# A one-column bias per row maximum: from GpSimd to VectorE

## The chip, the cores and the metric

The kernel runs on one core of a Trainium2 chip. The metric is the device time of one execution in microseconds (us). Ratios below are the mean time of one kernel's fast runs over that of the other's fast runs of the same rounds, so they are not quite the ratio of the medians quoted beside them. Engines: PE is TensorE (PEld its weight loads), DVE is VectorE, ACT is ScalarE, POOL is GpSimd, SP is SyncE, which issues most DMAs (388 of the 455 on the page of before; GpSimd 64).

## The reference

Attention over 8 batches, 8 heads, 576 rows and columns, head size 64, in which only scores within `tau` of the row's maximum count, followed by two matrix products with a hard-swish between them:

```python
scores = scale * q @ k.T
thresh = max(scores, axis=-1) - tau
scores = where(scores >= thresh, scores, -1e9)
attn   = exp(scores - max(scores)) / sum(...)
x      = attn @ v                          # to (4608, 512)
h      = x @ w_in
out    = (h * clip(h + 3, 0, 6) / 6) @ w_out
```

## The kernel before

A main loop of 144 slots works on two 128x576 score tiles per slot. In slot n the softmax of slot n runs beside the exponentials of slot n-1, one piece of the first matrix product, one of the second, and the scores of slot n+1. From slot 22 on the matrix products fill PE (97% busy from 100 to 500 us); slots 0 to 21 (here "the head") are attention alone.

```python
def sm_max(sl):                            # VectorE: copy out of PSUM with row maximum; then the bias
    ...
    for i, ps in enumerate(sl.tiles):
        nc.vector.tensor_scalar(out=sl.s[:, i, :]..., in0=ps[:, :, 0:HALF], scalar1=1.0, scalar2=None,
                                op0=Alu.mult, op1=Alu.max, accum_out=sl.m[:, i:i + 1])
        nc.gpsimd.tensor_scalar(out=sl.bias[:, i:i + 1], in0=sl.m[:, i:i + 1], scalar1=-scale, scalar2=tau,
                                op0=Alu.mult, op1=Alu.add)

def sm_mask(sl, i):                        # ScalarE: needs the bias
    nc.scalar.activation(out=s, in_=s, func=Act.Prelu, bias=sl.bias[:, i:i + 1], scale=scale, alpha=REJECT)

def sm_norm(sl):                           # GpSimd: two 128x576 normalizations, then a DMA transpose
    ...

for n, sl in enumerate(queue):             # one slot
    ...                                    # exponentials of slot n-1 (ScalarE)
    sm_max(sl)
    ...                                    # first product -> relu -> gate; reciprocal of n-1; second product
    for i in range(2):
        sm_mask(sl, i)
    ...                                    # transposes or attn @ v; scores of slot n+1
    sm_norm(prev)
    start(loads, 1)                        # q, k of later slots: issued by SyncE
    if n < 4 or n > 12:
        start(vcasts, 1)                   # one load of V:       issued by GpSimd
    if n > 3:
        start(casts, 1 if n < 24 else 2)   # pieces of the weights: issued by GpSimd
```

GpSimd's instructions start in the order of the program. There are two score banks in PSUM (one per tile) and one `h` bank: the next scores wait for this slot's maxima (PE sat idle 2.8 us for them in all), and the next piece of the first product waits for the gate (5.0 us).

Of the kernel before, what the change touches and what calls it, by code (L numbers as in the profile page):

```python
# [21 lines left out]
def kernel(  # L22
# [10 lines left out]
    nc = tc.nc  # L33
# [11 lines left out]
    scale = 1.0 / math.sqrt(D)  # L45
    tau = float(tau)
# [227 lines left out]
    def sm_max(sl):  # L274
        sl.s = s_pool.tile([P, 2, S], F32, tag="s", name="s")
        sl.m = stat_pool.tile([P, 2], F32, tag="m", name="m")
        sl.bias = stat_pool.tile([P, 2], F32, tag="bias", name="bias")
        sl.rsum = stat_pool.tile([P, 2], F32, tag="rsum", name="rsum")
        sl.rinv = stat_pool.tile([P, 2], F32, tag="rinv", name="rinv")
        for i, ps in enumerate(sl.tiles):  # L280
            nc.vector.tensor_scalar(out=sl.s[:, i, :].rearrange("p (a b) -> p a b", a=2), in0=ps[:, :, 0:HALF],  # L281
                                    scalar1=1.0, scalar2=None, op0=Alu.mult, op1=Alu.max,
                                    accum_out=sl.m[:, i:i + 1])
            nc.gpsimd.tensor_scalar(out=sl.bias[:, i:i + 1], in0=sl.m[:, i:i + 1], scalar1=-scale, scalar2=tau,  # L284
                                    op0=Alu.mult, op1=Alu.add)

    def sm_mask(sl, i):
# [142 lines left out]
    for quad in range(NQUAD):  # L430
        for slot in range(NSLOT):
            sl = Slot()
# [6 lines left out]
    for n, sl in enumerate(queue):  # L439
# [13 lines left out]
        if prev is not None:  # L453
            for i in range(2):
                sm_exp(prev, i)
        sm_max(sl)

        if slot != 8 and todo1:
# [148 lines left out]
```

## Time and profile before

| | |
|---|---|
| time | 560.16 us median of 4 (559.52 to 560.89) |
| profiled span | 558.7 us, granted clock 0.996 |
| PE, DVE, ACT, POOL busy | 95%, 76%, 84%, 55% |
| bias on GpSimd | 288 instructions of 189 ns |
| ScalarE's wait for it | 35.2 us |

The lines themselves stand in the prediction. Lines from the timeline have the columns: start, duration, engine and line, operation, names, shapes, and in brackets the idle time before it and what ended it.

### The profile page before, as it was taken

Reading aid. Unit: us, or ns where it says so; the run is one execution under the profiler, and the core shown is the slowest. Engines: PE = TensorE matmul, PEld = TensorE weight load, DVE = VectorE, ACT = ScalarE, POOL = GpSimd, SP = SyncE. Lnnn points to the kernel's source line nnn. Section 1 sums busy time; section 2 is a strip of 40 time slices with the busy share of each in tenths; the row PEclk is TensorE's granted clock in tenths of the full one; section 3 lists DMA queues with packets and bytes.
Section 4 is the critical chain, followed back from the end, with each engine's and each line's share of the span. In section 5 each row is a group of like instructions: output and inputs, shape, how many; then the busy total and the mean of one; then the engine's idle time right before and its main releaser. Section 6 shows DMA issues by size and latency. Waiting matters only on the chain.

```text
span 558.7 us, 11624 instructions
## 1 busy us (share of the span) xinstructions
PE 530.6 (95%) x3829; PEld 309.2 (55%) x3870; DVE 424.7 (76%) x1041; ACT 469.7 (84%) x999; POOL 305.3 (55%) x646
## 2 busy tenths in 40 slices
PE   8899798799999999999999999999999999999997
PEld 6655455555555555655555555655555565654663
DVE  3787686787878788887978788887978798883440
ACT  4899899798889999899898999899898999984440
POOL 2788878854556555755556555755556555561000
PEclk9999899999999999999999999999999999999999
DMA  5999979976789869978689889977689865454102
GB/s 121 137 120 173 196 128 190 204 142 126 137 158 152 152 136 157 178 149 146 130 148 152 173 131 160 175 147 147 131 145 166 150 144 114 100 109 94 38 20 76
DMA packets 286348, 77.52 MB, mean 139 GB/s; under 512 B 269264, under 2 KB 281808, under 8 KB 286288
## 3 DMA queue, kind: packets, MB, share of 16 engines
q1 hardware_dynamic: 267680, 67.47, 65.3%
q0 software_dynamic: 17408, 8.92, 13.6%
q8 instruction: 30, 0.49, 0.4%
q10 hardware_dynamic: 1200, 0.39, 0.3%
q14 instruction: 30, 0.25, 0.1%
HBM read 36.70 MB, written 9.44 MB: 83 GB/s over the span
## 4 chain that ended last, share of the span: by engine, by line
PE 55%; DVE 11%; ACT 8%; issue 4%; SPq 3%; DMA 2%; POOL 2%; DVEq 0%; POOLq 0%
PE h L357 17%; PE o L386 16%; PE s L260 15%; DVE s L281 5%; PE av L327 3%; ACT s L289 3%; ACT s L294 3%; DMA nq<-in_q_dram 2%; DVE g L374 2%; DVE r L368 2%; ACT r L366 1%; PE s L266 1%; PE tp L214 1%; SPq L310 1%; POOL pn L302 1%
## 5 line engine op out<-in xcount | busy, mean ns | idle before, releaser
L302 POOL TENSOR_SCALAR pn<-s,rinv 128x576 bf16<-128x576 f32 x288 | 211.6, 745 | 133.1 <-DVE rinv L297 57.3
L289 ACT ACTIVATE s<-s,bias 128x576 f32<-128x576 f32 x288 | 206.9, 766 | 36.3 <-POOL bias L284 35.2
L281 DVE TENSOR_SCALAR_CACHE_REDUCE s<-s 128x576 f32<-128x576 f32 x288 | 205.9, 752 | 40.3 <-PE s L260 29.9
L294 ACT ACTIVATE s<-s 128x576 f32<-128x576 f32 x288 | 192.7, 671 | 0.3
L260 PE MATMUL s<-kT,qT 64*128 64x288 f32 x1024 | 169.7, 430 | 5.1 <-DVE s L281 2.8
L357 PE MATMUL h<-xT,w_in_sb 128*128 128x320 bf16 (+1 forms) x1024 | 144.9, 287 | 5.9 <-DVE g L374 5.0
L386 PE MATMUL o<-w_out_sb,g 128*128 128x512 bf16 x535 | 133.5, 379 | 5.2 <-DVE osb L394 3.0
L357 PEld LDWEIGHTS <-w_in_sb 128*128 128x128 bf16 x1024 | 92.1, 97 | 68.9 <-issue 31.9
L374 DVE SCALAR_TENSOR_TENSOR g<-r,h 128x512 bf16<-128x512 f32 (+1 forms) x128 | 96.4, 755 | 41.7 <-ACT r L366 39.9
L260 PEld LDWEIGHTS s<-kT,qT 64*128 64x128 f32 x1024 | 93.7, 186 | 60.9 <-DVE s L281 24.0
L284 POOL TENSOR_SCALAR bias<-m 128x1 f32<-128x1 f32 x288 | 54.4, 189 | 66.6 <-DVE s L281 45.8
L386 PEld LDWEIGHTS <-g 128*128 128x128 bf16 x576 | 55.6, 98 | 57.4 <-issue 9.0
L366 ACT ACTIVATE r<-h,three 128x640 f32<-128x640 f32 (+1 forms) x74 | 54.4, 736 | 20.6 <-PE h L357 19.9
L294 ACT ACTIVATION_READ_ACCUMULATOR s<-s 128x1 f32 x288 | 54.2, 188 | 0.0
L368 DVE TENSOR_SCALAR r<-h 128x512 f32<-128x512 f32 (+1 forms) x54 | 40.5, 751 | 0.0
L394 DVE TENSOR_SCALAR osb<-o 128x512 f32<-128x512 f32 x31 | 21.0, 676 | 21.4 <-PE o L386 21.4
L327 PE MATMUL av<-pT,vm 128*64 128x512 bf16 x256 | 34.6, 393 | 2.0 <-ACT kT L204 2.0
L327 PEld LDWEIGHTS <-vm 128*64 128x64 bf16 x512 | 18.0, 111 | 25.3 <-issue 18.8
L297 DVE RECIPROCAL rinv<-rsum 128x2 f32<-128x2 f32 x144 | 23.0, 160 | 11.3 <-ACT s L294 10.5
L339 DVE CAST xT<-av 128x512 bf16<-128x512 f32 x32 | 21.8, 681 | 6.6 <-PE av L330 6.3
L281 DVE DVE_READ_ACCUMULATOR s<-s 128x1 f32 x288 | 23.9, 83 | 0.0
L266 PE MATMUL s<-kT,qT 64*64 64x288 f32 x256 | 20.1, 415 | 0.7 <-DVE s L281 0.7
(44 smaller groups left out, 241.4 us busy)
## 6 DMA issues: line engine op xcount, KB each, us to landing
km<-in_k_dram SPq DMA_DIRECT2D x64, 128.0 KB, 3.0
out_dram<-osb SPq DMA_DIRECT2D x31, 256.0 KB, 2.4
nq<-in_q_dram SPq DMA_DIRECT2D x96, 72.0 KB, 2.7
vm<-in_v_dram POOLq DMA_DIRECT2D x16, 256.0 KB, 5.6
w_in_sb<-in_moe_w_in_dram POOLq DMA_DIRECT2D x16, 128.0 KB, 4.3
w_out_sb<-in_moe_w_out_dram POOLq DMA_DIRECT2D x16, 128.0 KB, 4.5
pT<-pn SPq DMA_TRANSPOSE x119, 3.4
nq<-in_q_dram SPq DMA_DIRECT2D x14, 128.0 KB, 4.4
```

Source lines behind the costliest of these rows:

```text
L260: nc.tensor.matmul(tiles[a][:, hf, 0:HALF], qT_of(pair)[a * 64:(a + 1) * 64, t * P:(t + 1) * P], keys(pair, a, hf), start=True, stop=True)
L281: nc.vector.tensor_scalar(out=sl.s[:, i, :].rearrange("p (a b) -> p a b", a=2), in0=ps[:, :, 0:HALF], scalar1=1.0, scalar2=None, op0=Alu.m ...
L284: nc.gpsimd.tensor_scalar(out=sl.bias[:, i:i + 1], in0=sl.m[:, i:i + 1], scalar1=-scale, scalar2=tau, op0=Alu.mult, op1=Alu.add)
L289: nc.scalar.activation(out=s, in_=s, func=Act.Prelu, bias=sl.bias[:, i:i + 1], scale=scale, alpha=REJECT)
L294: nc.scalar.activation(out=s, in_=s, func=Act.Exp, accum_out=sl.rsum[:, i:i + 1])
L302: nc.gpsimd.tensor_scalar(out=pn[:, i, :], in0=sl.s[:, i, :], scalar1=sl.rinv[:, i:i + 1], scalar2=1.0, op0=Alu.mult, op1=Alu.mult)
L327: nc.tensor.matmul(ps[a * 64:(a + 1) * 64, :], vm[:, 2 * hp + a, c * D:(c + 1) * D], pT[:, 5 * a + c, cols], start=(c == 0), stop=False)
L357: nc.tensor.matmul(hps[:, n, 0:w], w_in_sb[:, ki, (ni + n) * P:(ni + n + 1) * P], xT[b][:, ki, c0:c0 + w], start=(ki == 0), stop=(ki == KI ...
L366: nc.scalar.activation(out=r, in_=hps, func=Act.Relu, bias=three[:])
L368: nc.vector.tensor_scalar(out=r, in0=hps, scalar1=3.0, scalar2=0.0, op0=Alu.add, op1=Alu.max)
L374: nc.vector.scalar_tensor_tensor(out=gbuf[:, ni:ni + 2, c0:c0 + w], in0=r, scalar=6.0, in1=hps, op0=Alu.min, op1=Alu.mult)
L386: nc.tensor.matmul(o_ps[0], gbuf[:, ni, mt * P:(mt + 1) * P], w_out_sb[:, ni, :], start=(ni == 0), stop=(ni == NI - 1))
```

## The change

Intent: ScalarE waits 35 us for a bias that GpSimd makes late, as it is often busy with a normalization: 116 of the 288 maxima were ready during one, and their bias started 0.69 us after the maximum had been read (median), instead of 0.09. VectorE has just made the maximum, so let it make the bias too.

```diff
-            nc.gpsimd.tensor_scalar(out=sl.bias[:, i:i + 1], in0=sl.m[:, i:i + 1], scalar1=-scale, scalar2=tau,
+            nc.vector.tensor_scalar(out=sl.bias[:, i:i + 1], in0=sl.m[:, i:i + 1], scalar1=-scale, scalar2=tau,
                                     op0=Alu.mult, op1=Alu.add)
```

## The prediction

> **What bounds the kernel now.** I read the page's busy shares first, then the table of stretches, then the costliest groups, then the chain of waits, and last a stretch of the timeline of one steady slot. A "slot" is one turn of the kernel's main loop: 144 of them, each with two 128x576 score tiles.
>
> ```profile
> PE 530.6 (95%) x3829; PEld 309.2 (55%) x3870; DVE 424.7 (76%) x1041; ACT 469.7 (84%) x999; POOL 305.3 (55%) x646
> ...
> PE 55%; DVE 11%; ACT 8%; issue 4%; SPq 3%; DMA 2%; POOL 2%; DVEq 0%; POOLq 0%
> ```
>
> TensorE (PE) is busy 95% of the span and holds 55% of the chain that ended last; VectorE (DVE) is second on that chain with 11%, about 61 us. The averages hide three stages, so I cut the span into the attention-only head, the mixed middle and the tail (columns: stretch, length, then busy us and instruction count of PE, PEld, DVE, ACT, POOL; clock; DMA share; GB/s).
>
> ```profile
> 24.00:80.00 56.00, 49.89 (x392) 29.26 (x390) 44.23 (x123) 50.57 (x113) 46.14 (x97) 0.97 1.01 153
> 100.00:500.00 400.00, 389.35 (x2848) 223.00 (x2886) 331.69 (x812) 364.43 (x785) 228.07 (x484) 1.00 0.83 146
> 510.00:559.00 49.00, 44.25 (x275) 25.23 (x275) 15.78 (x23) 14.61 (x21) 0.00 (x0) 0.99 0.14 49
> ```
>
> In the head PE is 89% busy, ScalarE (ACT) 90%, GpSimd (POOL) 82%. In the middle PE is 97% busy, ACT 91%, DVE 83%, POOL 57%. In the tail the changed line doesn't occur. So 400 of 559 us are a stage in which PE has almost nothing left to give, and in which DVE has about 17% of its time free.
>
> ```profile
> L281 DVE TENSOR_SCALAR_CACHE_REDUCE s<-s 128x576 f32<-128x576 f32 x288 | 205.9, 752 | 40.3 <-PE s L260 29.9
> L284 POOL TENSOR_SCALAR bias<-m 128x1 f32<-128x1 f32 x288 | 54.4, 189 | 66.6 <-DVE s L281 45.8
> L289 ACT ACTIVATE s<-s,bias 128x576 f32<-128x576 f32 x288 | 206.9, 766 | 36.3 <-POOL bias L284 35.2
> ```
>
> These are the row maximum, the bias and the mask. The bias costs 189 ns on POOL, and ACT's mask stood idle for it 35.2 us in all. By stage, adding up the idle times in the timeline: 8.9 us of it lie before 80 us, 2.6 between 80 and 100, about 23 in the middle.
>
> [...]each of the 288 bias instructions waits on DVE's own semaphore. What such a wait costs, the trace has: the DVE relu into r ends at 206.37 us and the gate that waits for it starts at 206.40, a gap of 0.03. [...]the 128x2 reciprocal shows 160 ns, and the next instruction starts 80 ns after it. [...]
>
> **The change part by part.** PE, ACT and SP keep their instructions and order. POOL loses 288 instructions, DVE gains 288.
>
> Removed: 288 x 189 ns = 54.4 us of POOL work, so POOL falls to about 251 us. POOL isn't the bound, but it is in order: a bias often sat behind a normalization. Two stretches show the hand-overs:
>
> ```profile
> 204.31 0.76 DVE L281 TENSOR_SCALAR_CACHE_REDUCE s<-s 128x576 f32<-128x576 f32 x1
> 205.00 0.08 DVE L281 DVE_READ_ACCUMULATOR s<-s 128x1 f32 x1
> 205.00 0.75 DVE L281 TENSOR_SCALAR_CACHE_REDUCE s<-s 128x576 f32<-128x576 f32 x1
> 205.68 0.08 DVE L281 DVE_READ_ACCUMULATOR s<-s 128x1 f32 x1
> 205.68 0.69 DVE L368 TENSOR_SCALAR r<-h 128x512 f32<-128x512 f32 x1
> 206.40 0.69 DVE L374 SCALAR_TENSOR_TENSOR g<-r,h 128x512 bf16<-128x512 f32 x1
> ...
> 51.31 0.46 POOL L284 TENSOR_SCALAR bias<-m 128x1 f32<-128x1 f32 x2
> 51.52 1.44 ACT L289 ACTIVATE s<-s,bias 128x576 f32<-128x576 f32 x2 [0.60 <-POOL bias L284]
> ```
>
> Look at the accumulator read: it and the next maximum start together at 205.00, so today it costs DVE nothing.
>
> Added on DVE, per bias: the accumulator read must now be over before the bias starts, 0.08 us; the wait, 0.03; then the bias itself. I take it at some 0.13 to 0.16 us (the reciprocal's 160 ns[...]) of which, as with the reciprocal, 0.08 overlap with the next instruction, so about 0.07 count. Sum 0.18 us per bias, 0.36 per slot, 288 x 0.18 = 52 us in all. As busy time the page should show some 0.15 each, 43 us, so DVE at about 468 us. The largest part isn't the instruction but the broken overlap.
>
> What it does in the head (22 slots of about 3 us): at 51.52 ACT had been idle 0.60 us for a bias whose first maximum was out at about 50.32; DVE would deliver it near 50.5, before ACT is free at 50.92. Nearly all of the 8.9 us of ACT's wait there goes. ACT is the tightest chain in the head, but PE (89%), POOL (82%) and the DMA engines (share 1.01) are close behind, and DVE gives back 0.36 per slot. I book a third to a half: -3 us, perhaps -1 to -6.
>
> What it does in the middle: the 23 us that ACT waits there buy almost nothing directly, since PE's own idle time from 100 to 500 us adds up to only 8 us. The cost is a delayed release: DVE frees the two score banks for the next scores, and the single h bank through the gate for the next first-layer product. I took, for every slot from 22 on, DVE's idle time in it (mean about 0.54 us; but under 0.35 in 38 of the last 103 slots, and near 0.2 for slots 4, 6 and 7 of a group of nine). Carrying a debt of 0.36 per slot, paid back from idle time, and letting PE lose whatever exceeds the slack between DVE's release and PE's use gives the loss. That slack I read off the timeline: from the gate's end to the next first-layer product it is 0.48 us in the middle case but under 0.1 in a fifth; from the last accumulator read to the next scores 0.55 in the middle and 0.21 at the low end. With a slack of 0.25 the loss is 5.5 us, with 0.5 it is 1.6; if only half of the idle time that DVE spends waiting for ACT's relu can be used, 9.2 and 5.3. I choose the middle of these four, +6. A second way agrees: DVE's 61 us on the chain are about 20 slots' worth of its 3 us, and 20 x 0.36 = 7.
>
> Tail: 0. Sum: 560.2 - 3 + 6 = 563; I add one for the fact that the count above lets late PE work never disturb ACT or the DMA transposes. 564 us, +0.7%.
>
> **The rivals.** First, ACT as the true bound: freed of 35 us of waits, the middle too would speed up, to 545 to 552. For it: mask and exp sit on long pieces of the chain in the head, and ACT is 91% busy. Against: PE at 97% in the middle can't take it up. Second, DVE becomes the bound: 83% plus 0.30 of a 3.45 us slot is 92%, plus the wait gaps 94%; with heavy slots next to one another PE would wait in most of them, giving 572 to 580. For it: on the chain there are runs of over 3 us of pure DVE work (maximum, relu, gate, reciprocal, output scaling). Against: the mean idle of 0.54 per slot is more than 0.36. Third, [...]if the one-element bias does lock against GpSimd, it would often meet a normalization of 745 ns, as that starts right after the reciprocal, just ahead of the next maximum. Up to 0.7 us each would block DVE itself, and the kernel would pass 600. [...]I give it 4%. Fourth, the whole is hidden: 558 to 562.
>
> **Range and chances.** The four middle estimates with the head's -1 to -6 span about 556 to 570; DVE's cost per bias could be 0.15 or 0.25, which widens it upwards. Range 555 to 577. Faster than 549: 0.03. Within 2%: 0.77. Slower than 571.4: 0.20, most of it from the second rival.
>
> **What would show it.** Right: the bias group on DVE with 288 instructions of 120 to 160 ns, the second maximum starting about 0.86 us after the first instead of 0.69, DVE near 468 us, POOL near 251, ACT's wait for the bias under 12 us, the head some 3 us shorter, and PE in the middle with 6 to 10 us more waits on DVE's maximum and gate. Wrong: if PE's waits in the middle don't grow, the slack was larger than I read; [...]if the middle gets shorter, ACT was the bound there.

## More of the kernel before

```profile
5.06 0.63 PE L214 MATMUL tp<-identf,km 128*128 128x128 f32 x4 [0.45 <-DMA km<-in_k_dram]
...
8.62 0.76 DVE L281 TENSOR_SCALAR_CACHE_REDUCE s<-s 128x576 f32<-128x576 f32 x1 [1.33 <-PE s L260]
...
9.48 0.19 POOL L284 TENSOR_SCALAR bias<-m 128x1 f32<-128x1 f32 x1 [8.17 <-DVE s L281]
...
10.40 0.93 POOL L122 DMA_DIRECT2D vm<-in_v_dram  x1
```

The first K arrives just before 5.06, the first row maximum starts at 8.62, and GpSimd stands 8.17 us at its first bias before it gets to issue the first load of V at 10.40.

## The result, and the profile after

568.28 us median of 4 (567.54 to 571.64) against 560.16; ratio 1.0156, 95% interval 1.0128 to 1.0185. The time lies in the predicted range and within the 2% band, but the loss is 1.6% where 0.7% had been forecast. A second set of runs of the same kernel (below) gave 1.0167.

Page of the changed kernel: busy shares, then engines on the chain that ended last.

```profile
PE 536.1 (95%) x3870; PEld 312.1 (55%) x3870; DVE 462.8 (82%) x1329; ACT 475.5 (84%) x999; POOL 250.5 (44%) x358
...
PE 62%; DVE 19%; ACT 7%; DMA 6%; issue 4%; POOL 1%; SPq 1%; DVEq 0%; POOLq 0%; ACTq 0%
```

VectorE has 38 us more busy time and GpSimd 55 us less, about as forecast. On the chain VectorE went from 11% to 19%, and DMA from 2% to 6%. (PE's busy time can't be compared to a per cent: the trace of before lacks 41 matmul records.)

The groups:

```profile
L281 DVE TENSOR_SCALAR_CACHE_REDUCE s<-s 128x576 f32<-128x576 f32 x288 | 215.4, 748 | 34.7 <-PE s L260 31.0
L289 ACT ACTIVATE s<-s,bias 128x576 f32<-128x576 f32 x288 | 214.3, 769 | 21.6 <-DVE bias L284 17.7
...
L284 DVE TENSOR_SCALAR bias<-m 128x1 f32<-128x1 f32 x288 | 44.3, 154 | 10.0
```

The bias takes 154 ns on VectorE (152 to 156 in all 288). ScalarE's wait for it halves, from 35.2 to 17.7 us, and does not vanish. One slot's hand-over on the timeline:

```profile
203.12 0.72 DVE L281 TENSOR_SCALAR_CACHE_REDUCE s<-s 128x576 f32<-128x576 f32 x1
...
203.77 0.08 DVE L281 DVE_READ_ACCUMULATOR s<-s 128x1 f32 x1
...
203.89 0.15 DVE L284 TENSOR_SCALAR bias<-m 128x1 f32<-128x1 f32 x1
203.96 0.75 DVE L281 TENSOR_SCALAR_CACHE_REDUCE s<-s 128x576 f32<-128x576 f32 x1
...
204.14 1.58 ACT L289 ACTIVATE s<-s,bias 128x576 f32<-128x576 f32 x2 [0.46 <-DVE bias L284]
```

The second maximum starts 0.84 us after the first; before it was 0.69. The accumulator read, which used to run beside the next maximum (both start at 205.00 in the prediction's lines), now ends first: at 203.85, with the bias at 203.89 and the next maximum at 203.96, 0.07 after the bias.

And the start, which the prediction had not thought of:

```profile
1.45 0.93 POOL L122 DMA_DIRECT2D vm<-in_v_dram  x1
...
7.05 1.09 PE L214 MATMUL tp<-identf,km 128*128 128x128 f32 x4 [2.43 <-DMA km<-in_k_dram]
...
12.37 0.76 DVE L281 TENSOR_SCALAR_CACHE_REDUCE s<-s 128x576 f32<-128x576 f32 x1 [1.80 <-PE s L260]
```

With no bias in GpSimd's queue, nothing holds the first load of V back: it is issued at 1.45 us instead of 10.40, at the same time as the first K and Q (from 0.74 us). PE waits 2.43 us for K instead of 0.45, then its transposes take 1.09 us instead of 0.63, and the first maximum starts at 12.37 us instead of 8.62: 3.75 us are lost before the first moved instruction has run.

To see where the rest went, I took from each trace when the first maximum of a slot starts, and subtracted the same of before. The five columns add up to the difference of the two profiled spans: at slot 0; gained or lost between slots 0 and 28; 28 and 40; 40 and 143; and after that. Each row is a single trace, so chance is in it, and the stretches before slot 40 show it; the stretch from 40 to 143 turns out to repeat within 0.15 us.

| trace (us against before) | start | 0-28 | 28-40 | 40-143 | end | span |
|---|---|---|---|---|---|---|
| changed kernel | +3.75 | -0.77 | +0.94 | +4.00 | -0.22 | +7.7 |
| changed kernel, second trace (run 12) | +4.57 | -1.39 | -0.64 | +4.02 | -0.22 | +6.3 |

So there are two large terms: a late start, and 4 us spread evenly over the mixed middle.

Theories. (A) VectorE's own cost explains the middle: the overlap of maximum and accumulator read, broken twice per slot. (B) The late start is GpSimd's queue: what held V back is gone. Rivals: the start is chance, or is made up later; the middle's loss comes not from VectorE's load but from a shifted phase in which DMAs collide.

### The profile page after: what moved, and what is told of

Its sections match the earlier page's. It is cut to its first block, busy times and chain, and to the rows that moved or that the text cites. A ratio compares the mean times of both kernels' runs of the same rounds, so it can differ in the third digit from the quotient of the medians.

```text
span 566.4 us, 11766 instructions
## 1 busy us (share of the span) xinstructions
PE 536.1 (95%) x3870; PEld 312.1 (55%) x3870; DVE 462.8 (82%) x1329; ACT 475.5 (84%) x999; POOL 250.5 (44%) x358
## 4 chain that ended last, share of the span: by engine, by line
PE 62%; DVE 19%; ACT 7%; DMA 6%; issue 4%; POOL 1%; SPq 1%; DVEq 0%; POOLq 0%; ACTq 0%
PE s L260 17%; PE h L357 17%; PE o L386 16%; DVE s L281 9%; PE av L327 4%; ACT s L289 3%; DVE g L374 2%; ACT s L294 2%; DMA pT<-pn 2%; DVE r L368 2%; DVE bias L284 2%; PE tp L214 2%; PE s L266 2%; DMA pR<-pn 1%; ACT r L366 1%
## 5 line engine op out<-in xcount | busy, mean ns | idle before, releaser
L281 DVE TENSOR_SCALAR_CACHE_REDUCE s<-s 128x576 f32<-128x576 f32 x288 | 215.4, 748 | 34.7 <-PE s L260 31.0
L289 ACT ACTIVATE s<-s,bias 128x576 f32<-128x576 f32 x288 | 214.3, 769 | 21.6 <-DVE bias L284 17.7
L260 PE MATMUL s<-kT,qT 64*128 64x288 f32 x1024 | 172.3, 430 | 4.9 <-DVE s L281 2.4
L386 PE MATMUL o<-w_out_sb,g 128*128 128x512 bf16 x576 | 140.9, 379 | 4.3 <-DVE osb L394 4.3
L260 PEld LDWEIGHTS s<-kT,qT 64*128 64x128 f32 x1024 | 95.8, 186 | 60.6 <-DVE s L281 19.1
L374 DVE SCALAR_TENSOR_TENSOR g<-r,h 128x512 bf16<-128x512 f32 (+1 forms) x128 | 96.2, 752 | 14.4 <-ACT r L366 10.1
L284 DVE TENSOR_SCALAR bias<-m 128x1 f32<-128x1 f32 x288 | 44.3, 154 | 10.0
L214 PE MATMUL tp<-identf,km 128*128 128x128 f32 x128 | 19.8, 278 | 2.4 <-DMA km<-in_k_dram 2.4
```

Of the source, the lines that this page charges most:

```text
L260: nc.tensor.matmul(tiles[a][:, hf, 0:HALF], qT_of(pair)[a * 64:(a + 1) * 64, t * P:(t + 1) * P], keys(pair, a, hf), start=True, stop=True)
L281: nc.vector.tensor_scalar(out=sl.s[:, i, :].rearrange("p (a b) -> p a b", a=2), in0=ps[:, :, 0:HALF], scalar1=1.0, scalar2=None, op0=Alu.m ...
L284: nc.vector.tensor_scalar(out=sl.bias[:, i:i + 1], in0=sl.m[:, i:i + 1], scalar1=-scale, scalar2=tau, op0=Alu.mult, op1=Alu.add)
L374: nc.vector.scalar_tensor_tensor(out=gbuf[:, ni:ni + 2, c0:c0 + w], in0=r, scalar=6.0, in1=hps, op0=Alu.min, op1=Alu.mult)
L386: nc.tensor.matmul(o_ps[0], gbuf[:, ni, mt * P:(mt + 1) * P], w_out_sb[:, ni, :], start=(ni == 0), stop=(ni == NI - 1))
```

## The experiments

All results are correct against the reference. Times beside "before" are of the same rounds; 15 kernels ran.

**1. Hold the V load back in the changed kernel.** The first V load moves one slot later, behind the first normalization:

```diff
-        if n < 4 or n > 12:
+        if 0 < n < 5 or n > 12:
             start(vcasts, 1)
```

> Changed kernel, but the first load of V is issued by GpSimd one slot later, behind the first normalization. Start theory (the removed bias instructions had held that load back; without them it is issued at 1.45 us instead of 10.40 and delays the first K and Q): the first row maximum is back at 8.6 us (changed kernel 12.4), and the time is about 564.5 (568.3 less 3.8). Rival (all of the loss is VectorE's, the late start is chance or is made up later): 567 to 568.5.

Measured: 566.8 us (563.9 to 570.1), ratio 1.0108 (1.0075 to 1.0140). The first maximum is back at 8.70 us, so (B)'s start is right. But only some 0.5% of the loss went, not 0.7%: this trace loses 4.42 us between slots 28 and 40 and again 4.05 from 40 on. The runs spread over 6 us, and the trace is of a slow one of them (569.1 us); the two that were granted the full clock took 563.9 and 564.1 us, where 564.5 had been expected. Something else sits in slots 28 to 40; run 6 shows what.

**2. Let the V load go early in the kernel before.** Nothing changes on VectorE; the load is issued ahead of slot 0's bias:

```diff
+        if n == 0:
+            start(vcasts, 1)
         sm_max(sl)
```
(and `n < 4` becomes `0 < n < 4`)

> Kernel before, bias on GpSimd as it was, but the first load of V is issued before the first bias instead of behind it. Start theory: first row maximum at 12.4 us instead of 8.6, time about 564 (560.2 plus 3.8), with nothing changed on VectorE. Rival (VectorE only): 560.2. If part of a late start is soaked up by the head, 561 to 563.

Measured: 563.8 us, ratio 1.0058 (1.0038 to 1.0078). The load alone slows a kernel that is otherwise the one before. In its trace:

```profile
1.45 0.93 POOL L122 DMA_DIRECT2D vm<-in_v_dram  x1
...
6.74 0.63 PE L214 MATMUL tp<-identf,km 128*128 128x128 f32 x4 [2.13 <-DMA km<-in_k_dram]
...
10.30 0.76 DVE L281 TENSOR_SCALAR_CACHE_REDUCE s<-s 128x576 f32<-128x576 f32 x1 [1.33 <-PE s L260]
```

This trace is of the fastest of the six executions (560.9 us; the others took 563.1 to 565.6), so it may show less than the usual cost. K is 1.7 us late here too, but the transposes still take 0.63 us. In the changed kernel the wait was 2.43 us and the transposes took 1.09: about half of its late start (1.99 of 3.75 us) is the wait for K, the other half is PE running at half pace after it. The wait did not slow PE down; PE had not been sped up yet: the warm-up transposes of the changed kernel start every 0.21 us both before the wait and after it, and every 0.11 once the full clock is recorded. In every trace those ahead of K run at half pace (14 in 3.1 to 3.25 us). The clock records in the traces, read directly, show the full clock first from 4.73 us in the kernel before and from 5.29 us here, but only from 10.87, 12.23 and 12.71 us in the three traces that load V early and move every bias (the two of the changed kernel and that of run 14). So in these traces PE starts at half pace, and the moment at which the full clock comes varies, from 4.2 to 12.71 us. In seven other traces the transposes are slow too, although K came on time, as here in run 7:

```profile
4.99 1.09 PE L214 MATMUL tp<-identf,km 128*128 128x128 f32 x4 [0.37 <-DMA km<-in_k_dram]
```

That alone costs up to 1.2 us: where V is held back, the column "start" of the table below rises from 0 to +1.2 as the full clock comes at 4.2 to 7.4 us. Whether the late K is also what delays the full clock beyond 10 us is not shown, nor what else sets that moment.

**3. VectorE's cost without its benefit.** GpSimd's bias stays in use; VectorE computes the same into a tile that nobody reads:

```diff
             nc.gpsimd.tensor_scalar(out=sl.bias[:, i:i + 1], ...)
+            nc.vector.tensor_scalar(out=sl.idle[:, i:i + 1], in0=sl.m[:, i:i + 1], ...)
```

> Kernel before with its bias on GpSimd in use, and beside it the same bias on VectorE into a tile that nobody reads. VectorE cost alone, without the earlier bias for ScalarE and without an earlier V load. VectorE theory: start unchanged, the middle (slot 28 on) longer by about 5 us as in the changed kernel, 565 to 566. Rival (the middle is longer because the earlier bias makes ScalarE and the DMA transposes run into something): about 560 to 561.

Measured: 569.5 us (569.3 to 569.7), ratio 1.0164. The start is at 8.66 us, and slots 40 to 143 lose 6.58 us. So (A) holds, and is larger than I said: VectorE's added work costs 6.6 us there, and the changed kernel gets 2.6 of them back, from its earlier bias, from GpSimd's shorter queue, or from both; no run separates these. Its rival, that the phase or the DMAs do it, falls for this stretch.

**4. VectorE only in the head.** `by = nc.vector if 0 < now < N1 else nc.gpsimd`, so slots 1 to 21.

> Bias on VectorE only in slots 1 to 21, where ScalarE waited for it and TensorE is not full; slot 0 and the mixed middle keep GpSimd. By my theory the start is as before, the head gains 1 to 2 us, the middle loses nothing: 558.5 to 559.5. Rival (the head has no gain, its other engines take the slack): 560.2. If the V loads in the head come in each other's way: over 561.

Measured: 561.7 us, ratio 1.0026 (1.0012 to 1.0041). A miss: the head does not gain. Whether it loses is open: five of the six runs were granted a clock of 0.993 or 0.994, the sixth, at 0.997 like before, took 560.4 us. (The trace has 1.07 us of the total at slots 28 to 40, where the clock is halved for 3.4 us, and nothing from 40 on.)

**5. Everything but slot 0.** `by = nc.vector if now > 0 else nc.gpsimd`; the first V load is again behind a GpSimd bias.

> Changed kernel, but slot 0 keeps its bias on GpSimd, so that the first V load is issued exactly where it was before (about 10.4 us). Start theory: first row maximum at 8.6 to 9.2 us; the start's cost is gone and what is left is VectorE's: head 0 to +1, middle +4 to +5, so 565 to 566. Rival (the start's delay was soaked up later, so that removing it saves little): 566.5 to 568.

Measured: 565.9 us (564.4 to 569.6), ratio 1.0106 (1.0077 to 1.0134), first maximum at 8.58 us, slots 40 to 143 at +4.12. As expected: about 0.5% of the loss was the start. Where the head's gain went is seen in the waits between 15 and 94 us. Before:

```profile
ACT s L289 <- POOL bias L284: 7.8, 15, 1.3
...
DVE s L281 <- PE s L260: 1.8, 4, 0.5
```

and with VectorE's bias, same start:

```profile
DVE s L281 <- PE s L260: 7.2, 9, 2.0
...
ACT s L290 <- DVE bias L285: 7.0, 9, 2.2
```

ScalarE's wait was in good part renamed, not removed: the bias is quick now, but the maximum ahead of it starts late, as VectorE waits 7.2 us for scores instead of 1.8. The traces of runs 9 and 4, which share this start, show 4.8 and 4.4 us of ScalarE's wait and 5.7 and 5.4 of VectorE's. That the scores come late because the longer VectorE slot frees their two banks late is not shown: PE's own wait for the maxima is 2.7 us here and was 2.8 before.

**6. VectorE only in the middle.** `by = nc.vector if now >= N1 else nc.gpsimd`.

> Bias on VectorE only from slot 22 on, on GpSimd before. The middle alone, with start and head as before: from slot 40 to 143 it should lose the 4.0 us that the changed kernel and its late-V version lost there, in all 564 to 565.5. If costs add, this and the head-only run (+1.4) make up the slot-0 run. Rival (the middle's loss comes from a shift of phase that the head brings in): under 562.

Measured: 567.8 us (565.7 to 570.3), ratio 1.0121. From slot 40 it loses 3.98 us as expected, but 5.68 between 28 and 40, so the costs of runs 4 and 6 do not add up to run 5. The trace shows the event (pR is the transposed remainder of a group of heads, made by a DMA):

```profile
101.80 3.60 SPq L311 DMA_TRANSPOSE pR<-pn  x1
...
112.30 0.42 PE L328 MATMUL ar<-pR,vm 128*64 128x64 bf16 x8 [4.14 <-DMA pR<-pn]
...
112.98 2.29 PE L260 MATMUL s<-kT,qT 64*128 64x288 f32 x8
...
115.20 2.31 PE L358 MATMUL h<-xT,w_in_sb 128*128 128x320 bf16 x8
```

The transpose is issued at 101.80 and lands at 112.30, 10.5 us later; the median of the 15 transposes of this kind is 4.6. In the kernel before the same one took 7.9 us and PE did not wait for it. These are the slots in which GpSimd issues two pieces of the weights per slot and the V of the next batch at once: DMA share 1.42 from 96 to 115 us (1.36 before). PE waits 4.14 us, then eight score matmuls take 2.29 us instead of 1.24: the granted clock is halved from 111.7 to 118.5 us. The table of all traces below shows that this one wait goes with the loss at slots 28 to 40.

**7. Both biases behind both maxima** (slot 0 on GpSimd):

```diff
-            nc.gpsimd.tensor_scalar(out=sl.bias[:, i:i + 1], ...)       # in the loop, behind each maximum
+        for i in range(2):                                              # behind the loop
+            nc.vector.tensor_scalar(out=sl.bias[:, i:i + 1], ...)
```

> As the slot-0 run, but both biases stand behind both maxima, instead of one behind each. Theory of the broken overlap (0.08 us accumulator read and 0.03 us wait exposed, 0.07 us the instruction itself): the first of the two waits for nothing, so VectorE pays about 0.07 + 0.18 = 0.25 us per slot, not 0.36, and the second maximum starts 0.69 us after the first again; the loss against before falls to about 0.6 to 0.7 of the slot-0 run's. Rival (what costs is the instruction and nothing else): the same as the slot-0 run. Against it stands that ScalarE's first mask gets its bias 0.7 us later.

Measured: 564.9 us, ratio 1.0084; slots 40 to 143 at -0.15, with 4.47 lost at slots 28 to 40 in a wait of 3.8 us for the same transpose. Its timeline:

```profile
213.56 0.08 DVE L281 DVE_READ_ACCUMULATOR s<-s 128x1 f32 x1
213.56 0.27 DVE L288 TENSOR_SCALAR bias<-m 128x1 f32<-128x1 f32 x2
213.90 0.69 DVE L378 SCALAR_TENSOR_TENSOR g<-r,h 128x512 bf16<-128x512 f32 x1
```

The first bias starts together with the accumulator read of the second maximum: it waits for nothing, as its own maximum was read 0.7 us ago. The same two instructions take about 0.18 us of a slot instead of 0.36 (in another slot the next instruction follows 0.18 after that read), and the steady loss is gone, not two thirds of it as I had said. Order alone decides between 4 us and none. ScalarE waits 20.8 us for the bias in this stretch, as before (20.2), so that wait as such need not cost anything.

**8. One 128x2 bias behind both maxima** (slot 0 on GpSimd): `nc.vector.tensor_scalar(out=sl.bias[:], in0=sl.m[:], ...)`.

> As the slot-0 run, but one 128x2 bias behind both maxima. Without a lock[...]: instruction of about 155 ns, VectorE pays 0.18 us per slot, half of the slot-0 run's loss, 562.5 to 563.5. With the lock[...]: the instruction starts late or lasts up to 750 ns whenever a normalization runs, GpSimd's normalizations get gaps, and the time is over 572.

Measured: 561.0 us (558.9 to 567.7; the slowest is not in the ratio), ratio 1.0018 (0.9986 to 1.0050); slots 40 to 143 at +0.93. No catastrophe, but some of the biases are held up beside GpSimd's work. Durations (minimum, median, maximum in ns), and one of the long ones beside GpSimd's normalization:

```profile
L288 DVE TENSOR_SCALAR bias<-m x143: 168/170/405, 12.4 to 499.2; 128x2 f32<-128x2 f32 x143
```

```profile
100.60 1.46 POOL L306 TENSOR_SCALAR pn<-s,rinv 128x576 bf16<-128x576 f32 x2
...
101.81 0.28 DVE L288 TENSOR_SCALAR bias<-m 128x2 f32<-128x2 f32 x1
```

The bias ends at 102.09, right after the normalization (102.06). Of the 143, 27 took over 250 ns; 14 of these started with 0.25 us or more of a normalization left and end within 0.03 us of its end; the other 13 lie over a DMA that GpSimd is issuing. The delay shows as a longer VectorE instruction, not as idle time ahead of it: the 27 start 0.03 to 0.04 us after the accumulator read. Eight that started in the last 0.14 us of a normalization were not stretched. The 128x1 bias of the changed kernel ran 110 times during a normalization and never took over 156 ns. The delay is cheap here because 121 of the 143 start while no normalization runs.

**9. to 11. Take the late transpose away.** The second weight matrix is loaded two pieces a slot from slot 18 instead of 24, so that the dense loads are over before slot 27:

```diff
-            start(casts, 1 if n < 24 else 2)
+            start(casts, 1 if n < 18 else 2)
```

Run 9, in the kernel of run 5:

> The slot-0 run (VectorE's bias from slot 1, start as before), with the second weight matrix loaded two pieces a slot from slot 18 instead of 24, so that the dense loads are over before slot 27, where the transposes of the remainder land late and TensorE waits for them. Accident theory (the spread between runs and 1 to 5 us of loss at slots 28 to 40 are a one-time wait for that transpose with a halved TensorE clock after it): the loss at slots 28 to 40 falls to under 1 us, runs agree within 1 us at a clock of 0.999 or more, about 564.5. From slot 40 the loss stays at 4 us. Rival (the stage's loss is VectorE's load): no change, 564.4 to 569.6.

Measured: 563.3 us (562.4 to 563.8, and one run at 567.2), ratio 1.0054. No wait for that transpose; slots 28 to 40 at -1.57, 40 to 143 at +4.12.

Run 10, in the kernel before:

> The same earlier weights in the kernel before, as a control: it shows no wait for that transpose in its trace, so 559.5 to 561. If the earlier weights alone change the time by over 1.5 us, the comparison of the run beside it has to be taken against this kernel.

Measured: 559.9 us (558.8 to 560.0) against 560.9, ratio 0.9977 (0.9965 to 0.9990). Slots 28 to 40 at -1.62 here too. It is the only kernel whose interval lies below 1.

Run 11, in the kernel of run 8:

> The one 128x2 bias with the earlier weights. If the two slow runs of six of the one-wide kernel (565.8 and 567.7, clock 0.994) were that accident, all runs fall to 558 to 561, about 559.5; this may be the fastest kernel of the study. Rival (its spread has another cause): some runs over 565 again.

Measured: 561.8 us (560.0 to 563.0), ratio 1.0012. The runs above 565 are gone, the time I had named was not reached.

**12. The changed kernel again.**

> The changed kernel once more, for the cost of its start beside the slot-0 run and its own spread. If the late start is the rule and not chance, its first row maximum stands at 10 us or later again (8.6 in kernels with the load held back), and the time is 567.5 to 570. If the start is back at about 8.7 us, the late start of the first profile was chance.

Measured: 570.1 us (566.8 to 573.8), ratio 1.0167 (1.0134 to 1.0199), first maximum at 13.19 us. The late start is the rule. The changed kernel also spreads by over 1%, which before does not.

**13. Both biases behind both maxima, weights early:** runs 7 and 9 combined.

> Both biases on VectorE behind both maxima (slot 0 on GpSimd), weights early. Its first version lost 4.5 us at slots 28 to 40 only, and 0.1 us less than nothing from slot 40 on. Theory (the steady cost is the overlap broken twice a slot, and the late transpose is separate): no wait for that transpose, slot 40 to 143 at 0 +-0.5 against before, 557 to 560 us in all, level with or below the kernel before with early weights (559.9). Rival (the order costs as the other one does, and the first trace was luck): 563.

Measured: 560.7 us (557.4 to 564.3), ratio 0.9998 (0.9965 to 1.0030); slots 40 to 143 at -0.17. The steady cost is gone for the second time; it is level with before, and no faster. Against its control, run 10 (0.9977), it is 0.2% slower.

**14. The changed kernel with early weights.**

> The changed kernel with early weights, slot 0 on VectorE too. Start theory: first row maximum at 12 to 13 us again and 3 to 4 us over the slot-0 run with early weights (563.3): 566 to 567.5. Rival (the late start is soaked up by the head): 563 to 564.5.

Measured: 569.4 us (563.0 to 572.6; the slowest is not in the ratio), ratio 1.0133 (1.0090 to 1.0175), first maximum at 13.26 us. Against run 9 (1.0054) the start is worth 0.8%, in runs whose middle is the same; in runs 5 and 12 it was 0.5 to 0.6%. The profiled execution was a slow one, so of its trace only the start and the steady stretch (+4.00) are used. The run of 563.0, at the full granted clock, has no trace.

**15. Bias on both engines, weights early.**

> Bias on both engines, GpSimd's in use, with early weights. VectorE's cost alone: slot 40 to 143 at +6.6 again, 566 to 567.5 against 559.9 of the kernel before with early weights. If the benefit of the earlier bias is real, it is 2 to 3 us over the slot-0 run with early weights (563.3). Rival (the idle GpSimd work costs nothing and the earlier bias is worth nothing): 563.3.

Measured: 569.8 us, ratio 1.0155; slots 40 to 143 at +6.53. Over run 9 it is 1.0%, more than the 2 to 3 us I expected: the early bias and the shorter queue of GpSimd together are worth 2.4 us of it from slot 40 on; the rest of the difference lies in the head (+2.9 here, -1.0 in run 9, one trace each), where this trace has a stretch at half clock and that of run 9 has none.

All traces in one table (us against before; the last column is PE's idle wait for the transpose at slots 28 to 40, from the waits between 90 and 145 us):

| kernel | start | 0-28 | 28-40 | 40-143 | PE waits for pR |
|---|---|---|---|---|---|
| changed | +3.75 | -0.77 | +0.94 | +4.00 | 1.6 |
| 12. changed again | +4.57 | -1.39 | -0.64 | +4.02 | 0.9 |
| 14. changed, weights early | +4.64 | (slow) | (slow) | +4.00 | none |
| 1. V held back | +0.08 | +0.22 | +4.42 | +4.05 | 3.3 |
| 5. all but slot 0 | -0.04 | +0.45 | +2.08 | +4.12 | 1.9 |
| 9. same, weights early | +0.50 | -0.96 | -1.57 | +4.12 | none |
| 6. middle only | +0.39 | +0.27 | +5.68 | +3.98 | 4.1 |
| 3. on both engines | +0.04 | +1.10 | +0.87 | +6.58 | none |
| 15. same, weights early | +1.11 | +2.93 | -0.90 | +6.53 | none |
| 7. behind both | +1.01 | -1.78 | +4.47 | -0.15 | 3.8 |
| 13. same, weights early | +0.55 | +0.93 | -2.14 | -0.17 | none |
| 8. one 128x2 | -0.02 | -1.56 | -1.35 | +0.93 | 0.6 |
| 11. same, weights early | +0.01 | +1.91 | -1.71 | +0.90 | none |
| 2. before, V early | +1.68 | -1.27 | +0.01 | +0.03 | none |
| 4. head only | +0.52 | -0.62 | +1.07 | -0.31 | none |
| 10. before, weights early | +1.18 | -0.07 | -1.62 | +0.02 | none |

The fourth column is 3.98 to 4.12 us in all seven traces with VectorE's bias alone behind each maximum, and follows only how the bias is made. The third follows the wait for the late transpose. The second goes largely with something else: stretches of 3.41 us in which PE is granted half its clock (some last twice that, as the 6.8 in run 6). The nine traces without one up to slot 28 (in runs 4 and 10 one begins there, within 0.3 us of it) lie at -1.8 to +1.1 us (median about -1.0); the kernel before and five others have one and lie at 0 to +2.9, and runs 6 and 14 have two. Compared without such a stretch, the six with VectorE's bias in the head have -0.6 to -1.8, runs 2 and 10, with GpSimd's, -1.3 and -0.1, and run 3, with both, +1.1: no trace shows the 3 us of gain.

Such a stretch also came without a long wait ahead of it. In run 1 the clock is halved at 72.42 us (columns as in the prediction's table of stretches; the clock stands after the counts of the five engines):

```profile
69.01:72.42 3.41, 2.62 (x16) 1.27 (x15) 3.20 (x12) 3.15 (x7) 2.78 (x5) 1.00 1.30 173
72.42:75.83 3.41, 3.41 (x17) 1.56 (x19) 1.89 (x6) 2.93 (x8) 2.39 (x4) 0.50 1.01 196
```

PE had been busy for 2.62 of the 3.41 us ahead, and its longest wait there was 0.36 us. The spread of the timed runs goes with the same thing. In run 12 the two runs at a granted clock of 1.0 took 566.8 and 568.4 us, the one at 0.991 took 573.8; runs 1, 5, 8 and 14 spread in the same way. Runs at 0.999 or more alone give 566.8 to 568.4 us for the changed kernel and 563.9 to 564.8 for runs 1 and 5, so the start is worth 3 to 4 us, as (B) says.

How the 4 us come about in the steady stretch is seen in the waits from slot 40 to 143. Before:

```profile
ACT s L289 <- POOL bias L284: 20.2, 46, 1.5
...
ACT r L366 <- PE h L357: 9.6, 21, 0.9
...
PEld L357 <- DVE g L374: 4.4, 7, 0.8
```

and after:

```profile
ACT r L366 <- PE h L357: 19.2, 34, 1.4
...
PEld L357 <- DVE g L374: 11.8, 20, 1.0
...
ACT s L289 <- DVE bias L284: 6.8, 19, 0.5
```

ScalarE's wait for the bias fell by 13.4 us, and its wait for the first product rose by 9.6. PE's weight loads for that product wait 11.8 us for VectorE's gate instead of 4.4 (14.4 with the bias on both engines, 5.6 with both behind both maxima): the gate comes late, the single `h` bank is freed late, and PE, which has little slack (97% busy from 100 to 500 us before), starts the product late.

## Why the prediction was wrong, point by point

- **VectorE's cost per bias, 0.18 us, mostly the broken overlap: right.** The second maximum starts 0.84 to 0.88 us after the first (forecast 0.86), the wait costs 0.04, busy time is 462.8 us (forecast 468), GpSimd 250.5 (251). That the bias itself would take 0.13 to 0.16 us, a little less than the reciprocal's 160 ns, was the estimate; it took 154 ns. In run 7, which gives the overlap back, VectorE pays half of this per slot, and the steady loss is gone.
- **The middle, +6: right in kind, a little too high.** From slot 22 to 143 the changed kernel lost 4.4 us (7.92 at slot 143 less 3.54 at slot 22). It is the difference of two terms: VectorE's load costs 6.6 us from slot 40 on, and 2.6 come back. The prediction had "the 23 us that ACT waits there buy almost nothing". The 2.6 us are a gain that it left out, if they come from the bias and not from GpSimd's shorter queue; run 7 speaks for the queue, but this stays open.
- **The head, -3: wrong.** The step was "Nearly all of the 8.9 us of ACT's wait there goes". From 15 to 94 us it was 7.8; with VectorE's bias and the same start it was 7.0, 4.8 and 4.4 (runs 5, 9 and 4), as the maximum itself came later. Over the whole run 17.7 us of the wait were left, where under 12 had been forecast. The head-only run took 1.0026 of the time before where it should have gained.
- **The start: the term that is missing from the sum.** This is the step that failed most: moving the bias was taken to change GpSimd's busy time and the moment of the bias, and not when GpSimd issues its DMAs. The prediction looked at what stood ahead of the bias in GpSimd's queue ("a bias often sat behind a normalization") and not at what stood behind it. (Even in its own example, the bias at 51.31 us, GpSimd had been issuing DMAs, at 49.90 and 50.69, and not normalizing.) The first bias was the gate that kept a V load out of the way of the first K. Opening it cost 3.75 to 4.6 us at the first maximum in three traces, and 0.5 to 0.8% (3 to 4.5 us) in timed runs.
- **Spread:** not foreseen. The wait for one transpose, with the halved clock around it, makes up to 5.7 us in a trace; in the changed kernel's own traces it is small. Runs with early weights still spread (563.0 to 572.6 us in run 14), in step with the granted clock; what halves the clock in the head is open.
- **The rivals:** ScalarE as the bound, a lock of the one-element bias against GpSimd and a hidden change all fall. The one-element bias took 152 to 156 ns in all 288 cases, 110 of them during a normalization; the 128x2 bias of run 8 was stretched in 27 of 143, to at most 405 ns. Why the two differ is not shown.

By the first trace: 3.75 (start) - 0.77 (slots 0 to 28) + 0.94 (28 to 40) + 4.00 (40 to 143) - 0.22 = 7.7 us, against 0 - 3 + 6 + 1 = 4 in the prediction. The misses are in the first two; the middle, on which most of the working was spent, is not where it failed.

## What to carry to other kernels

Before an instruction leaves an in-order queue, look at what stands behind it: its wait may be the only thing that holds a DMA out of the way of a critical one (here it held the first load of V from 1.45 to 10.40 us, and the first maximum came at 8.62 instead of 12.37). In this kernel a tiny instruction that reads what the one before it wrote cost the overlap of the two on top of its own time (the second maximum started 0.84 to 0.88 us after the first instead of 0.69), so try to put it one instruction later, where its wait is already met (run 7: -0.15 us from slot 40 on instead of +4.12). And when a change makes run times spread, look at the granted clock of each run and for stretches in which PE's clock is halved, before averaging them into the cost.
